# A gated linear-attention scan feeding a rational-activation MLP: one activation-table set, heads in pairs, other PSUM buffers

## The chip, the cores and the metric

The kernel runs on one core of a Trainium2 chip. A core has TensorE (PE, with its weight loads shown as PEld), VectorE (DVE), ScalarE (ACT), GpSimd (POOL) and SyncE (SP), which here only issues DMAs. The metric is the device time of one launch in microseconds; less is better.

## The reference

Inputs are `q`, `k`, `v`, `f_logit`, each of shape (4, 8, 768, 48) (batch B, heads H, sequence S, head width D), and the weights of an MLP with 384 inputs, 2048 inner and 384 outer columns.

```python
f = 1.0 / (1.0 + np.exp(-f_logit))
for t in range(S):
    state = f[:, :, t, :, None] * state + np.einsum('bhd,bhe->bhde', k[:, :, t], v[:, :, t])
    y[:, :, t] = np.einsum('bhd,bhde->bhe', q[:, :, t], state)
...
h = x @ w_in
P = a[0] + a[1] * h + a[2] * h2 + a[3] * h3          # h2 = h*h, h3 = h2*h
Q = 1.0 + np.abs(b[0]) * np.abs(h) + np.abs(b[1]) * h2
g = P / (Q + 1e-06)
out = g @ w_out
```

`x` is `y` with its heads side by side: 3072 tokens of 384 columns.

## The kernel before

The sequence is cut into NC = 6 chunks of C = 128 steps. A chunk is one attention stage over the 8 heads, then one expert stage on its 4 x 128 = 512 tokens. (The MLP is called the expert stage here.)

**Attention, per head.** `q`, `k`, `f_logit` are loaded from the queue of SP and `v` from that of POOL, all four batches side by side (BD = 192 columns). ACT forms `sig` (L104) and its logarithm `lsig` (L106). PE multiplies `lsig` by a triangular matrix U, a running sum over time, into `csT`, a part of the PSUM tile `psA` (L112); ACT takes its exponential with either sign, `AT` (L115) and `AinvT` (L117). DVE and POOL scale `q` and `k` with them (`qt_n` L120, `kt_n` L122); PE transposes both into `psB` (L126, L128, eight in all); DVE copies the results out (`qt_d` L131, `kt_d` L133). PE makes four column sums for the last decay (L136), of which ACT takes the exponential `alast` (L140); the scores (L144), which DVE masks (`sc_sb` L149); y from the masked scores and from the old state (L153, L157), which ACT copies out (`y_sb` L162) and SP stores to the HBM tensor `xT`; and `sv`, k times v (L168). DVE adds it to the state (`stmp` L173) and scales by `alast` (`state` L176). `csT`, the column sums and `sv` share the one buffer of `psA`.

**Expert stage, per chunk.** `xc` is read back from `xT` in three loads. For each of the KF = 16 blocks `m` of the inner columns, PE makes `h_ps` (L188, three matmuls), DVE casts it to `hb` (L192) and squares it (L194, shown as h), ACT makes `habs` (L196) and `pA` (L198), POOL makes `pB` (L201), DVE makes t (L204) and `Pp` (L206), POOL makes q (L208), DVE makes `Qq` (L211), ACT makes `lnQ` (L213) and `Qinv = exp(-lnQ)` (L215), and DVE makes `gall` (L216). Then, for each batch `sub`, 16 matmuls of `gall` with `w_out` go to `o_ps` (L220), ACT copies them out (L224) and SP stores them.

**Order.** The loops are unrolled. A scheduler at build time orders each engine's instructions, by priorities and by the buffers that each pool has; each engine then runs its own list in that order. So work of the next chunk can stand among that of this one. ACT holds one set of function tables at a time; where a function is not in the set, a table load (ACT_TABLE_LOAD) stands before it.

Of the kernel before, what the change touches and what calls it, by code (L numbers as in the profile page):

```python
# [8 lines left out]
F32 = mybir.dt.float32  # L9
BF16 = mybir.dt.bfloat16  # L10
# [5 lines left out]
def kernel(  # L16
# [12 lines left out]
    nc = tc.nc  # L29
# [4 lines left out]
    BC = B * C  # L34
    d_model = H * D
# [13 lines left out]
    for bb in range(B):  # L49
# [16 lines left out]
                                            ap=[[0, P]] + list(moe_b.ap)))  # L66
    babs = w_pool.tile([P, 2], F32)
    nc.scalar.activation(babs, b_sb, AF.Abs)

    with tc.tile_pool(name="attn_sb", bufs=3) as sb, \  # L70
         tc.tile_pool(name="attn_bf", bufs=3) as bf, \
         tc.tile_pool(name="ps_a", bufs=1, space=bass.MemoryType.PSUM) as ps_a, \
         tc.tile_pool(name="ps_b", bufs=1, space=bass.MemoryType.PSUM) as ps_b, \
         tc.tile_pool(name="ps_sc", bufs=1, space=bass.MemoryType.PSUM) as ps_sc, \
         tc.tile_pool(name="ps_y", bufs=1, space=bass.MemoryType.PSUM) as ps_y, \
         tc.tile_pool(name="ps_h", bufs=2, space=bass.MemoryType.PSUM) as ps_h, \
         tc.tile_pool(name="ps_o", bufs=2, space=bass.MemoryType.PSUM) as ps_o, \
# [8 lines left out]
      for c in range(NC):  # L86
        t0 = c * C
        for h in range(H):
            state = states[h]
            qn = sb.tile([C, BD], F32, tag="qn")  # L90
            kn = sb.tile([C, BD], F32, tag="kn")
            vn = bf.tile([C, BD], BF16, tag="vn")
            fn = sb.tile([C, BD], F32, tag="fn")
            nc.sync.dma_start(out=qn.rearrange("t (b d) -> t b d", b=B),
                              in_=q[:, h, t0:t0 + C, :].rearrange("b t d -> t b d"))
            nc.sync.dma_start(out=kn.rearrange("t (b d) -> t b d", b=B),
                              in_=k[:, h, t0:t0 + C, :].rearrange("b t d -> t b d"))
            nc.gpsimd.dma_start(out=vn.rearrange("t (b d) -> t b d", b=B),  # L98
                                in_=v[:, h, t0:t0 + C, :].rearrange("b t d -> t b d"))
            nc.sync.dma_start(out=fn.rearrange("t (b d) -> t b d", b=B),  # L100
                              in_=f_logit[:, h, t0:t0 + C, :].rearrange("b t d -> t b d"))

            sig = sb.tile([C, BD], F32, tag="sig")
            nc.scalar.activation(sig, fn, AF.Sigmoid)  # L104
            lsig = bf.tile([C, BD], BF16, tag="lsig")
            nc.scalar.activation(lsig, sig, AF.Ln)  # L106

            psA = ps_a.tile([C, 512], F32, tag="psA")
# [147 lines left out]
```

## Time and profile before

| | us |
|---|---|
| median of 6 runs (lowest to highest) | 875.47 (873.52 to 876.59) |
| the profiled execution, its time | 875.5 |
| its span from first to last instruction | 873.7 |
| ACT busy | 755.8 |
| PE / DVE / POOL busy | 441.9 / 363.3 / 219.6 |

The span is what the trace shows; 1.8 us of the time lie around it. An engine's busy time is a mean over two kinds of stage that alternate six times, so the stages are read apart. In a row of the timeline the first number is the start in us from the span's start, the second the length; in square brackets stands how long the engine had been idle before it and who ended that. A name such as `hb<-h_ps` says what is written from what.

### The profile page before, as it was taken

To read this page: it belongs to the slowest core of one execution; us is meant where nothing else is said; L and a number is where in the kernel's file an instruction comes from. 1 tells how busy PE (TensorE), PEld (TensorE's weight loads), DVE (VectorE), ACT (ScalarE), POOL (GpSimd) and SP (SyncE) were. 2 spreads that over 40 slices of the span, in tenths; PEclk is the share of its full clock that TensorE was granted. 3 is DMA by queue.
4 is the path that set the end of the run, shared out by engine and by line. 5 is a ranking of instruction groups with operands and counts; after the bars stand their busy time and mean duration, and the time that the engine had idled before them with its cause. 6 is when DMAs were issued, how large, how long until landed. Compare 5 with 4: busy or idle time off the path is not lost. (4 is left out here: it accounts for less than half of the span.)

```text
span 873.7 us, 7492 instructions
## 1 busy us (share of the span) xinstructions
PE 441.9 (51%) x2041; PEld 195.8 (22%) x2064; DVE 363.3 (42%) x873; ACT 755.8 (87%) x1012; POOL 219.6 (25%) x306
## 2 busy tenths in 40 slices
PE   0466544276644256664336664426665425755424
PEld 0243210043310024310013421103331102421001
DVE  0233655323554423365423364542345452345441
ACT  4888999868999968899978899996899996539994
POOL 3112432111432201252201243210233220224220
PEclk9999755565655565555556555556555556555556
DMA  9744100034300024400013420002430001200000
GB/s 161 102 65 68 20 0 1 17 73 61 48 2 0 0 55 70 69 8 0 0 29 66 66 40 1 0 0 66 68 51 3 1 0 48 39 19 0 1 0 36
DMA packets 127114, 29.59 MB, mean 34 GB/s; under 512 B 121569, under 2 KB 126689, under 8 KB 127073
## 3 DMA queue, kind: packets, MB, share of 16 engines
q1 hardware_dynamic: 99264, 23.61, 13.4%
q0 software_dynamic: 27808, 5.51, 7.3%
q8 instruction: 16, 0.26, 0.1%
q14 instruction: 26, 0.20, 0.1%
HBM read 27.53 MB, written 7.08 MB: 40 GB/s over the span
## 5 line engine op out<-in xcount | busy, mean ns | idle before, releaser
L220 PE MATMUL o_ps<-w_out_sb,gall 128*128 128x384 bf16 x384 | 116.7, 443 | 226.2 <-DVE gall L216 226.0
L188 PE MATMUL h_ps<-xc,w_in_sb 128*128 128x512 bf16 x265 | 125.7, 603 | 55.5 <-DVE hb L192 48.7
L201 POOL TENSOR_SCALAR pB<-hb,a_sb 128x512 bf16<-128x512 bf16 x96 | 78.4, 817 | 183.5 <-DVE Pp L206 143.7
L213 ACT ACT_TABLE_LOAD x90 | 115.5, 1283 | 1.6
L215 ACT ACT_TABLE_LOAD x90 | 115.5, 1283 | 1.6
L220 PEld LDWEIGHTS <-gall 128*128 128x128 bf16 x384 | 34.4, 112 | 336.1 <-DVE gall L216 315.1
L208 POOL TENSOR_SCALAR q<-h,babs 128x512 bf16<-128x512 bf16 x96 | 69.9, 729 | 112.5 <-DVE h L194 109.7
L98 POOL DMA_DIRECT2D vn<-in_v_dram x48 | 38.5, 802 | 230.3 <-PE y_ps L157 225.0
L216 DVE TENSOR_TENSOR gall<-Pp,Qinv 128x512 bf16<-128x512 bf16 x96 | 40.8, 425 | 116.1 <-ACT Qinv L215 115.7
L211 DVE TENSOR_TENSOR Qq<-q,habs 128x512 bf16<-128x512 bf16 x96 | 41.5, 433 | 95.9 <-ACT habs L196 95.3
L198 ACT ACTIVATE pA<-hb,a_sb 128x512 bf16<-128x512 bf16 x96 | 76.6, 798 | 0.0
L196 ACT ACTIVATE habs<-hb,babs 128x512 bf16<-128x512 bf16 x96 | 67.8, 707 | 6.0 <-DVE hb L192 6.0
L131 DVE COPY qt_d<-psB 48x512 bf16<-48x512 bf16 x48 | 20.0, 417 | 117.4 <-PE psB L128 83.7
L192 DVE CAST hb<-h_ps 128x512 bf16<-128x512 f32 x96 | 65.0, 683 | 6.7 <-PE h_ps L188 6.5
L126 PE MATMUL psB<-ident,qt_n 128*48 128x128 bf16 x192 | 49.0, 311 | 35.1 <-DVE qt_n L120 35.1
L153 PE MATMUL y_ps<-sc_sb,vn 128*48 128x128 bf16 x192 | 55.1, 287 | 19.1 <-DVE sc_sb L149 19.1
L188 PEld LDWEIGHTS <-w_in_sb 128*128 128x128 bf16 x288 | 35.5, 128 | 117.0 <-issue 114.8
L106 ACT ACT_TABLE_LOAD x47 | 60.3, 1283 | 0.8
L213 ACT ACTIVATE lnQ<-Qq 128x512 bf16<-128x512 bf16 x96 | 59.8, 628 | 1.0
L215 ACT ACTIVATE Qinv<-lnQ 128x512 bf16<-128x512 bf16 x96 | 59.8, 628 | 1.0
L104 ACT ACT_TABLE_LOAD x45 | 57.7, 1283 | 0.8
L157 PE MATMUL y_ps<-qt_d,state 48*48 48x128 bf16 x192 | 56.2, 293 | 0.0
(47 smaller groups left out, 702.3 us busy)
## 6 DMA issues: line engine op xcount, KB each, us to landing
qn<-in_q_dram SPq DMA_DIRECT2D x48, 96.0 KB, 2.6
kn<-in_k_dram SPq DMA_DIRECT2D x48, 96.0 KB, 2.5
fn<-in_f_logit_dram SPq DMA_DIRECT2D x48, 96.0 KB, 2.1
out_dram<-o_sb SPq DMA_DIRECT2D x24, 192.0 KB, 1.9
vn<-in_v_dram POOLq DMA_DIRECT2D x48, 48.0 KB, 2.9
xT_bridge<-y_sb SPq DMA_DIRECT2D x48, 48.0 KB, 2.3
xc<-xT_bridge SPq DMA_DIRECT2D x18, 128.0 KB, 2.6
w_in_sb<-in_moe_w_in_dram POOLq DMA_DIRECT2D x1, 1536.0 KB, 11.2
```

The lines of the kernel that those rows point to most:

```text
L104: nc.scalar.activation(sig, fn, AF.Sigmoid)
L106: nc.scalar.activation(lsig, sig, AF.Ln)
L157: nc.tensor.matmul(y_ps[:, b * C:(b + 1) * C], state[:, b * D:(b + 1) * D], qt_d[:, b * C:(b + 1) * C], start=False, stop=True)
L188: nc.tensor.matmul(h_ps, w_in_sb[:, kk, m * P:(m + 1) * P], xc[:, kk].rearrange("p b s -> p (b s)"), start=(kk == 0), stop=(kk == KD - 1))
L192: nc.vector.tensor_copy(hb, h_ps)
L196: nc.scalar.activation(habs, hb, AF.Abs, scale=babs[:, 0:1])
L198: nc.scalar.activation(pA, hb, AF.Identity, scale=a_sb[:, 3:4], bias=a_sb[:, 2:3])
L201: nc.gpsimd.tensor_scalar(pB, hb, a_sb[:, 1:2], a_sb[:, 0:1], op0=ALU.mult, op1=ALU.add)
L208: nc.gpsimd.tensor_scalar(q1, h2, babs[:, 1:2], 1.0 + 1e-6, op0=ALU.mult, op1=ALU.add)
L213: nc.scalar.activation(lnQ, Qq, AF.Ln)
L215: nc.scalar.activation(Qinv, lnQ, AF.Exp, scale=-1.0)
L220: nc.tensor.matmul(o_ps, gall[:, mm, sub * C:(sub + 1) * C], w_out_sb[:, mm, :], start=(mm == 0), stop=(mm == KF - 1))
```

## The change

1. One table set. Before the first activation `preload_act_table_set("natural_log_exp_and_others")` is called. `sig` is now exp(-f) and `lsig` is Ln(sig + 1), which is minus the old `lsig`; the signs of the three exponentials that follow are turned. Sigmoid is gone. The compiled program has 1 ACT_TABLE_LOAD row, where it had 315.
2. Heads in pairs. `qn`, `kn`, `vn`, `fn`, `sig`, `lsig`, `csT`, `AT`, `AinvT`, `qt_n`, `kt_n` are made for HG = 2 heads at once (GD = 384 columns); the loads stay one per head. The rest stays per head, in an inner loop over `j`.
3. Buffers. `attn_sb` has 2 instead of 3 buffers (of pairs); `AT` and `AinvT` move to a pool of their own with 3. `csT` has a PSUM bank of its own; the column sums and `sv` share a new one, `psS`. `ps_o` goes from 2 buffers to 1.
4. A constant `one_eps` is written and not used.

```diff
+    HG = 2
+    GD = HG * BD
...
+    nc.scalar.preload_act_table_set("natural_log_exp_and_others")
...
-    with tc.tile_pool(name="attn_sb", bufs=3) as sb, \
+    with tc.tile_pool(name="attn_sb", bufs=2) as sb, \
+         tc.tile_pool(name="attn_hb", bufs=3) as hsb, \
...
-         tc.tile_pool(name="ps_a", bufs=1, space=bass.MemoryType.PSUM) as ps_a, \
+         tc.tile_pool(name="ps_cs", bufs=1, space=bass.MemoryType.PSUM) as ps_cs, \
...
+         tc.tile_pool(name="ps_sv", bufs=1, space=bass.MemoryType.PSUM) as ps_sv, \
...
-         tc.tile_pool(name="ps_o", bufs=2, space=bass.MemoryType.PSUM) as ps_o, \
+         tc.tile_pool(name="ps_o", bufs=1, space=bass.MemoryType.PSUM) as ps_o, \
...
-        for h in range(H):
+        for hg in range(H // HG):
...
-            nc.scalar.activation(sig, fn, AF.Sigmoid)
+            nc.scalar.activation(sig, fn, AF.Exp, scale=-1.0)
...
-            nc.scalar.activation(lsig, sig, AF.Ln)
+            nc.scalar.activation(lsig, sig, AF.Ln, bias=1.0)
...
-            nc.scalar.activation(AT, csT, AF.Exp, scale=1.0)
+            nc.scalar.activation(AT, csT, AF.Exp, scale=-1.0)
...
+            for j in range(HG):
+                h = h0 + j
+                jo = j * BD
...
+                psS = ps_sv.tile([D, 512], F32, tag="psS")
+                alast_ps = psS[:, 0:B]
+                sv_ps = psS[:, 256:256 + BD]
```

Three places in the compiled order. First ACT, in the middle of an expert stage; one `m`, before:

```order
L213 ACT_TABLE_LOAD
L213 ACTIVATE lnQ<-Qq 128x512
L196 ACTIVATE habs<-hb,babs 128x512
L215 ACT_TABLE_LOAD
L215 ACTIVATE Qinv<-lnQ 128x512
L198 ACTIVATE pA<-hb,a_sb 128x512
```

And after, with one row of the next `m` behind it (L227 was L213, L210 was L196, L229 was L215, L212 was L198):

```order
L227 ACTIVATE lnQ<-Qq 128x512
L210 ACTIVATE habs<-hb,babs 128x512
L229 ACTIVATE Qinv<-lnQ 128x512
L212 ACTIVATE pA<-hb,a_sb 128x512
L227 ACTIVATE lnQ<-Qq 128x512
```

The four activations keep their order; the two loads are gone.

Second DVE, in the same place; before:

```order
L204 TENSOR_TENSOR t_974<-pA,h_966 128x512
L192 CAST hb<-h_ps 128x512
L206 TENSOR_TENSOR Pp<-t_974,pB 128x512
L211 TENSOR_TENSOR Qq<-q_1005,habs 128x512
L194 TENSOR_TENSOR h_1020<-hb 128x512
L216 TENSOR_TENSOR gall<-Pp,Qinv 128x512
```

After (L218, L206, L220, L225, L230, L208 for the same six operations):

```order
L218 TENSOR_TENSOR t_1000<-pA,h_992 128x512
L206 CAST hb<-h_ps 128x512
L220 TENSOR_TENSOR Pp<-t_1000,pB 128x512
L225 TENSOR_TENSOR Qq<-q_1031,habs 128x512
L208 TENSOR_TENSOR h_1046<-hb 128x512
L230 TENSOR_TENSOR gall<-Pp,Qinv 128x512
```

The six operations and their count stay; in most of the later blocks h and `gall` stand the other way round.

Third PE, in an attention stage, from the last score matmul of a head on; before:

```order
L144 MATMUL sc_ps<-qt_d,kt_d 128x128
L112 LDWEIGHTS U
L112 MATMUL psA<-lsig,U 128x192
L153 LDWEIGHTS vn
L153 MATMUL y_ps<-sc_sb,vn 48x128
L157 LDWEIGHTS state
L157 MATMUL y_ps<-qt_d,state 48x128
```

After:

```order
L159 MATMUL sc_ps<-qt_d,kt_d 128x128
L138 LDWEIGHTS qt_n
L138 MATMUL psB<-ident,qt_n 48x128
L140 LDWEIGHTS kt_n
L140 MATMUL psB<-ident,kt_n 48x128
L183 LDWEIGHTS kt_n
L183 MATMUL psS<-vn,kt_n 48x48
```

Before, y of the same head followed the scores, after the running sum of the next one. Now the transposes of the next head and `sv` of this one stand between the scores and y. In later chunks the column sums stand there too, just ahead of `sv`. Also on PE, one output matmul (L234, before L220) stands behind each block's three `h_ps` matmuls inside the expert stage, where two stood; 48 of a chunk's 64 follow after the stage, in groups of 16 among the matmuls of the next heads, where 32 did.

More of the change, by code (lines that the diff above doesn't have):

```diff
@@ L120 @@
             nc.vector.tensor_mul(qt_n, qn, AT)
[L121 removed]
+            kt_n = bf.tile([C, GD], BF16, tag="kt_n")
             nc.gpsimd.tensor_mul(kt_n, kn, AinvT)
[L124 to L129 removed]
```

151 lines of the change are left out of this document (76 added, 75 removed).

## The prediction

> **What bounds the kernel now.** I read the windows first, with one window on an attention stage (from the last `gall` of a chunk to the first `hb` of the next) and one on the expert stage that follows; the columns are stretch, length, busy time of PE, PEld, DVE, ACT, POOL, then granted clock, DMA share, GB/s. Above them stands the first line of the page.
>
> ```profile
> PE 441.9 (51%) x2041; PEld 195.8 (22%) x2064; DVE 363.3 (42%) x873; ACT 755.8 (87%) x1012; POOL 219.6 (25%) x306
> ...
> 452.40:509.70 57.30, 40.15 (x255) 23.52 (x257) 17.48 (x45) 45.04 (x73) 10.36 (x15) 0.56 0.43 71
> 509.70:592.50 82.80, 33.45 (x85) 8.96 (x87) 42.90 (x101) 81.91 (x99) 25.30 (x33) 0.52 0.03 4
> ```
>
> In the expert stage ACT is busy 81.91 of 82.80 us and nothing else above 42.90: ACT bounds it. In the attention stage ACT has 45.04 of 57.30, PE 40.15: neither is full, so a chain binds it. One chunk takes 140.1. The groups by line say what ACT does (count | busy, mean ns | idle before):
>
> ```profile
> L213 ACT ACT_TABLE_LOAD x90 | 115.5, 1283 | 1.6
> L215 ACT ACT_TABLE_LOAD x90 | 115.5, 1283 | 1.6
> ...
> L106 ACT ACT_TABLE_LOAD x47 | 60.3, 1283 | 0.8
> ...
> L104 ACT ACT_TABLE_LOAD x45 | 57.7, 1283 | 0.8
> ...
> L115 ACT ACT_TABLE_LOAD x41 | 52.6, 1283 | 0.7
> ```
>
> These five lines are 313 loads of 1.283 us, 402 of ACT's 755.8 us. The timeline of ACT (start, length) shows one `m` of the expert loop, and that of DVE the same loop later:
>
> ```profile
> 422.01 1.28 ACT L213 ACT_TABLE_LOAD   x1
> 423.30 0.63 ACT L213 ACTIVATE lnQ<-Qq 128x512 bf16<-128x512 bf16 x1
> 423.84 0.71 ACT L196 ACTIVATE habs<-hb,babs 128x512 bf16<-128x512 bf16 x1
> 424.56 1.28 ACT L215 ACT_TABLE_LOAD   x1
> 425.86 0.63 ACT L215 ACTIVATE Qinv<-lnQ 128x512 bf16<-128x512 bf16 x1
> 426.39 0.80 ACT L198 ACTIVATE pA<-hb,a_sb 128x512 bf16<-128x512 bf16 x1
> 427.21 1.28 ACT L213 ACT_TABLE_LOAD   x1
> ```
> ```profile
> 535.73 0.42 DVE L204 TENSOR_TENSOR t<-pA,h 128x512 bf16<-128x512 bf16 x1 [0.28 <-ACT pA L198]
> 536.08 0.69 DVE L192 CAST hb<-h_ps 128x512 bf16<-128x512 f32 x1
> 536.68 0.42 DVE L206 TENSOR_TENSOR Pp<-t,pB 128x512 bf16<-128x512 bf16 x1
> 538.36 0.42 DVE L211 TENSOR_TENSOR Qq<-q,habs 128x512 bf16<-128x512 bf16 x1 [1.27 <-ACT habs L196]
> 538.70 0.42 DVE L194 TENSOR_TENSOR h<-hb 128x512 bf16<-128x512 bf16 x1
> 540.23 0.42 DVE L216 TENSOR_TENSOR gall<-Pp,Qinv 128x512 bf16<-128x512 bf16 x1 [1.11 <-ACT Qinv L215]
> ```
>
> ACT repeats every 5.20 us (422.01 to 427.21) without a gap, two loads in each; DVE waits for it twice (1.27 before `Qq`, 1.11 before `gall`).
>
> The attention stage, one head, and then two `state` rows of the last chunk:
>
> ```profile
> 480.77 0.28 PE L136 MATMUL psA<-onesc_g,lsig 128*48 128x1 bf16 x4
> 481.44 0.30 PE L128 MATMUL psB<-ident,kt_n 128*48 128x128 bf16 x1 [0.39 <-POOL kt_n L122]
> 482.17 0.37 PE L168 MATMUL psA<-vn,kt_n 128*48 128x48 bf16 x4
> 482.42 0.42 DVE L131 COPY qt_d<-psB 48x512 bf16<-48x512 bf16 x1 [1.89 <-PE psB L128]
> 483.22 0.60 PE L144 MATMUL sc_ps<-qt_d,kt_d 48*128 48x128 bf16 x4 [0.68 <-DVE kt_d L133]
> 483.86 0.69 DVE L149 TENSOR_TENSOR sc_sb<-sc_ps,mask 128x512 bf16<-128x512 f32 x1 [0.44 <-PE sc_ps L144]
> 486.51 0.35 DVE L176 TENSOR_TENSOR state<-stmp,alast 48x192 bf16<-48x192 f32 x1 [1.96 <-PE y_ps L157]
> ...
> 763.40 0.35 DVE L176 TENSOR_TENSOR state<-stmp,alast 48x192 bf16<-48x192 f32 x1 [1.96 <-PE y_ps L157]
> 768.83 0.35 DVE L176 TENSOR_TENSOR state<-stmp,alast 48x192 bf16<-48x192 f32 x1 [1.96 <-PE y_ps L157]
> ```
>
> A head runs PE, DVE, PE, DVE in turn: transposes from 481.44 (end at 482.17, where L168 starts), copies, scores from 483.22, mask 483.86, y until 486.5. DVE waits for y 1.96 us with nothing to do, and PE waits for the copies and the mask. The `state` rows, one per head, come 5.43 apart in the last chunk; in the window above, seven of them (six of the chunk's heads and the first of the next) and the output matmuls share 57.3.
>
> **The change, part by part.**
>
> *Table loads.* The order has 315 load rows before and 1 after. ACT's `m` without its two loads is 5.20 - 2 x 1.28 = 2.64; since `lnQ` to `habs` steps 0.54 for a length of 0.63 where no load follows, two more such overlaps would give 2.45. I take 2.5 for ACT alone. The load row shows no drain around it: `pA` ends at 427.19, the load starts at 427.21, and `lnQ` starts 0.01 after the load before it. The Trainium skill (ScalarE: Activation LUTs, What ACT_TABLE_LOAD costs) puts a switch at about 2.66 us, 1283 ns of load and a drain of about 1380 ns. By it 314 removed loads would be worth 835 us of ACT, by the row 403; the trace agrees with the 1283 and shows no drain, so the row counts.
>
> *What is late next in the expert loop: DVE.* Six DVE operations per `m`, in the new order `t, hb, Pp, Qq, gall, h`. Start-to-start steps where DVE did not wait: t to hb 0.35, hb to Pp 0.60, Qq to h 0.34; the other three as the last. Sum 0.35 + 0.60 + 4 x 0.34 = 2.31. This is below ACT's 2.5. But POOL runs `pB` and `q` under it, and where DVE has no gaps the two disturb each other (first the spread of `pB`, ns min/median/max, then the start of an expert stage):
>
> ```profile
> L201 POOL TENSOR_SCALAR pB<-hb,a_sb x96: 752/762/1375, 89.9 to 848.3; 128x512 bf16<-128x512 bf16 x96
> ...
> 510.52 1.92 POOL L201 TENSOR_SCALAR pB<-hb,a_sb 128x512 bf16<-128x512 bf16 x2 [2.51 <-DVE hb L192]
> 512.42 1.77 POOL L208 TENSOR_SCALAR q<-h,babs 128x512 bf16<-128x512 bf16 x2
> ...
> 512.58 0.79 DVE L204 TENSOR_TENSOR t<-pA,h 128x512 bf16<-128x512 bf16 x1
> ```
>
> `pB` alone takes 0.76; two of them take 1.92 here, two `q` 1.77, and the DVE `t` under them 0.79 where its row above has 0.42. So a collision costs DVE about 0.4 and POOL up to 0.4. It does not touch `hb`, whose length stays 0.69 (it reads PSUM), so one of the two POOL operations of an `m` fits under `hb`'s 0.60; the other meets four back-to-back DVE operations. I charge one full collision, 0.48 (0.4, and 0.08 for the handoff): 2.31 + 0.48 = 2.8 per `m`. Bounds: 2.5 (no collision; ACT paces), and 3.2 (five DVE operations, 5 x 0.34, and two POOL operations, 2 x 0.76, never at once). The middle is nearest the row of 510.52.
>
> The Trainium skill (SBUF — State Buffer, Who interferes with whom) has this as an exclusive lock: a DVE instruction with two SBUF inputs and a GpSimd one that reads SBUF block each other in full. By that the bound of 3.2 would be the time per `m`; the rows agree with blocking, and its median of 762 ns says that a half-busy DVE leaves POOL its gaps.
>
> Sixteen `m` are 44.8 (16 x 2.8). Filling and draining the pipeline costs about 2.5 (a lone `hb`, `h`, `q` before the first `Qq`; `lnQ`, `Qinv`, `gall` after the last). By the order two heads of the next chunk now run inside the loop (one before); on a DVE without gaps each costs two copies at 0.42, the mask's 0.69, `stmp` and `state` at 0.35, 2.2 less 0.2 of overlap, so 4.0. Expert stage: 51, for 82.8.
>
> *Heads in pairs, transposes ahead.* PE's order becomes scores, transposes of the next head, `alast`, `sv`, y. The two copies (0.42 each) then lie under y, the mask (0.69) under the transposes. What remains in line: scores 0.60, eight transposes 0.83 (seven took 0.73), `alast` 0.28, its way through ACT about 0.3, `sv` 0.37, y 1.96, half a `csT` about 0.2: 4.54. I take 4.5. Bounds: 4.0, with the ACT handoff and drains hidden, and 5.4, the row of the last chunk, where the same serial chain ran with ACT's waits smallest. The pairing halves four ACT operations and `qt_n`/`kt_n` in number at twice the width; ACT and POOL are off the path here, so nothing. Eight loads per pair instead of four per head are the same bytes; DMA is at 0.43 of 57.3 us, that is 24.6 us of work in a stage of 43, still under it. New waits: a pair's `sig` needs both heads' `fn`, hidden by the second buffer; the store of y stands on SP behind loads that wait for a pair's buffer (rival C).
>
> *`ps_o` with one buffer.* Only one quarter of the output matmuls runs inside the expert loop; 48 instead of 32 come after it, and each 16 wait for ACT's copy of the previous 16.
>
> ```profile
> 454.55 6.45 PE L220 MATMUL o_ps<-w_out_sb,gall 128*128 128x384 bf16 x32
> ...
> 779.86 1.29 DVE L192 CAST hb<-h_ps 128x512 bf16<-128x512 f32 x2 [5.56 <-PE h_ps L188]
> ```
>
> The 32 took 6.45, 0.20 each; 48 are 9.7, and I charge 11 for a lower clock when heads stand between them. The separate `psS` bank lets `csT` go early; its cover is y. The last head's way through HBM to the first `hb` (5.56 of DVE idle in the last chunk) stays; I charge 5, since one next head fits into it.
>
> Attention stage: six heads 27 + 11 + 5 = 43, for 57.3.
>
> *Sum.* The start is bound by the first loads: the first `state` at 29.94, the first `hb` at 89.07, the last `gall` at 861.08.
>
> ```profile
> 29.94 0.35 DVE L176 TENSOR_TENSOR state<-stmp,alast 48x192 bf16<-48x192 f32 x1 [1.96 <-PE y_ps L157]
> ...
> 89.07 1.29 DVE L192 CAST hb<-h_ps 128x512 bf16<-128x512 f32 x2 [0.25 <-PE h_ps L188]
> ...
> 861.08 0.42 DVE L216 TENSOR_TENSOR gall<-Pp,Qinv 128x512 bf16<-128x512 bf16 x1 [3.00 <-ACT Qinv L215]
> ```
>
> After: 30 + 7 heads x 4.5 + 5.6 + 2 for the second head's loads = 69. Then 51; four chunks of 43 + 51 = 376; the last chunk, with no heads to interleave, 41 + 47 = 88; and the tail, 873.7 - 861.5 = 12.2 plus 16 matmuls of 0.20 = 15. Sum 599; the profiled execution took 875.5 for a span of 873.7, so 1.8 on top: 601. The median of the runs is 875.47, the same, so no shift.
>
> **The rivals.**
>
> A. ACT paces: POOL's two operations slip into waits of DVE and no collision costs. For it: ACT at 2.5 leaves DVE 0.2 of slack per `m`. Against: the row of 510.52. 96 `m` x 0.3 less: 572.
>
> B. The collision in full, 3.2 per `m`: 96 x 0.4 more: 639. For it: `pB` up to 1375 ns. Against: those are the extremes.
>
> C. Heads do not get below 5.4, because loads or the `alast`-`sv` handoff hold PE: 48 x 0.9 more: 644. For it: SP takes loads and stores in one row, and `alast` now sits between transposes and `sv`. Against: in this trace DMA is at 0.43.
>
> D. PE gets its full clock in the attention stage. The windows above have 0.56 and 0.52; PE would be busy 4.0 of 4.5. If PE's share shrank by a quarter: 48 x 1.0 less, 553. The Trainium skill (TensorE: Matmul & The Clock Gate, Part 1) has the clock released by one busy window of about 3.4 us. Against: the denser output matmuls release it here, the heads never did.
>
> E. The change does not do what it says, the functions keep switching tables: the expert stage stays at 82.8 and only heads gain, 601 + 6 x 32 = 793. Against: one load row in the order.
>
> F. Slower than before: on SP a pair's y stores stand behind loads whose buffers only a later pair frees, and PE stands still until `y_sb` is free, once for each of the 24 pairs. It decides from 274 / 24 = 11.4 us per pair, more than the pair's 9. At 12 us: 889. Against: three buffers for `y_sb`.
>
> **How the numbers follow.** My case 0.46, A 0.17, B 0.13, C 0.14, D 0.05, E 0.02, F 0.03. Predicted 601, its own range 580 to 625. With A, B and C inside, and the outer bounds of the head (4.0: 24 less) and of the ACT pace: 550 to 660, which leaves out E, F and the far ends of the others. 0.2% is about what a measurement of this kernel can tell. Faster by over 0.2%: all but F and a remainder, 0.96; same 0.01; slower 0.03.
>
> **What would show it.** ACT_TABLE_LOAD x1 and ACT busy near 335 (755.8 less 403 less some 20 for halved counts). `t` to `t` near 2.8 on DVE, its idle before `Qq` or `gall` small, `pB` and `q` means over 0.9 on POOL; 2.5 with ACT gapless would be A. `state` rows about 4.5 apart; 5.4 with PE waiting for ACT or a DMA would be C. First `hb` near 69. The prediction is wrong if a transfer, not an engine, ends the waits in the attention stage, or if the 48 output matmuls hold up the heads by much more than 11.

## The result, and the profile after

The kernel after takes 546.11 us (median of 8 runs, 544.57 to 547.70), the kernel before 875.57 in the same comparison (16 runs): a ratio of 0.624, 95% interval 0.6231 to 0.6249. The prediction was 601 with a range of 550 to 660: the direction and the terms of the expert stage held; the time came out 55 us lower, just under the range. The profiled execution has a span of 544.6 us.

The page of the kernel after, busy time by engine:

```profile
PE 393.0 (72%) x2022; PEld 182.5 (33%) x2040; DVE 365.7 (67%) x850; ACT 323.6 (59%) x602; POOL 267.0 (49%) x282
```

Its groups of instructions (count | busy, mean ns | idle before and what ended it):

```profile
L215 POOL TENSOR_SCALAR pB<-hb,a_sb 128x512 bf16<-128x512 bf16 x96 | 120.8, 1258 | 81.3 <-DVE hb L206 46.8 <-DVE Pp L220 33.4 <-DVE gall L230 0.8
...
L222 POOL TENSOR_SCALAR q<-h,babs 128x512 bf16<-128x512 bf16 x96 | 82.1, 856 | 6.0 <-DVE h L208 6.0
...
L218 DVE TENSOR_TENSOR t<-pA,h 128x512 bf16<-128x512 bf16 x96 | 60.5, 631 | 3.6 <-ACT pA L212 3.6
L227 ACT ACTIVATE lnQ<-Qq 128x512 bf16<-128x512 bf16 x96 | 60.0, 628 | 26.9 <-DVE Qq L225 26.6
...
L69 ACT ACT_TABLE_LOAD x1 | 1.3, 1283 | 0.7 <-PEq L254 0.7
```

One table load is left, ACT's busy time has fallen from 755.8 to 323.6, and no engine is above 72%. `t` on DVE now takes 631 ns on the mean, `pB` on POOL 1258; and ACT waits 26.6 us in all for DVE's `Qq`. Those three say that DVE paces the expert loop, held up by POOL. One `m` in the timeline of DVE, then the same of POOL, shows it (start, length):

```profile
260.45 0.68 DVE L206 CAST hb<-h_ps 128x512 bf16<-128x512 f32 x1
261.05 0.41 DVE L220 TENSOR_TENSOR Pp<-t,pB 128x512 bf16<-128x512 bf16 x1
261.38 0.41 DVE L225 TENSOR_TENSOR Qq<-q,habs 128x512 bf16<-128x512 bf16 x1
261.72 0.41 DVE L230 TENSOR_TENSOR gall<-Pp,Qinv 128x512 bf16<-128x512 bf16 x1
262.05 0.41 DVE L208 TENSOR_TENSOR h<-hb 128x512 bf16<-128x512 bf16 x1
262.39 0.83 DVE L218 TENSOR_TENSOR t<-pA,h 128x512 bf16<-128x512 bf16 x1
263.13 0.68 DVE L206 CAST hb<-h_ps 128x512 bf16<-128x512 f32 x1
```
```profile
260.23 0.85 POOL L222 TENSOR_SCALAR q<-h,babs 128x512 bf16<-128x512 bf16 x1
261.64 1.31 POOL L215 TENSOR_SCALAR pB<-hb,a_sb 128x512 bf16<-128x512 bf16 x1 [0.55 <-DVE Pp L220]
262.92 0.85 POOL L222 TENSOR_SCALAR q<-h,babs 128x512 bf16<-128x512 bf16 x1
```

From `hb` to `hb` it is 2.68 us here; the median from `t` to `t` is 2.69. `pB` starts while DVE is in `Qq` and lasts through `gall` and `h`; `t`, which starts under it, takes 0.83; `q` then runs under `hb`. One DVE operation per `m` loses 0.41.

The windows, an expert stage and the attention stage behind it (the columns as before):

```profile
163.90:214.20 50.30, 33.36 (x111) 11.31 (x113) 46.09 (x105) 41.15 (x71) 36.05 (x35) 0.53 0.13 19
214.20:244.20 30.00, 28.48 (x206) 16.40 (x207) 14.26 (x34) 10.39 (x26) 7.04 (x9) 0.78 0.61 106
```

PE is busy 28.48 of 30.00 us in the attention stage, at a granted clock of 0.78 (before: 40.15 of 57.30, at 0.56). Last, `state` and the first `hb` of two chunks on DVE:

```profile
231.66 0.35 DVE L191 TENSOR_TENSOR state<-stmp,alast 48x192 bf16<-48x192 f32 x1 [1.75 <-PE y_ps L172]
...
234.75 0.35 DVE L191 TENSOR_TENSOR state<-stmp,alast 48x192 bf16<-48x192 f32 x1 [0.64 <-PE y_ps L172]
...
237.95 0.35 DVE L191 TENSOR_TENSOR state<-stmp,alast 48x192 bf16<-48x192 f32 x1 [0.86 <-PE y_ps L172]
...
242.15 0.35 DVE L191 TENSOR_TENSOR state<-stmp,alast 48x192 bf16<-48x192 f32 x1 [1.53 <-PE y_ps L172]
...
244.19 1.29 DVE L206 CAST hb<-h_ps 128x512 bf16<-128x512 f32 x2 [0.56 <-PE h_ps L202]
...
483.46 1.29 DVE L206 CAST hb<-h_ps 128x512 bf16<-128x512 f32 x2 [5.52 <-PE h_ps L202]
```

The first three `state` rows are 3.1 and 3.2 apart, the fourth 4.2. Before the first `hb` DVE idles 0.56 us in this chunk and 5.52 only in the last, which has no next heads to run.

Stage by stage, summed over the chunks (first `hb` to last `gall`; last `gall` to next first `hb`; the tail is what follows the last `gall`):

| us | start | 6 expert stages | 5 attention stages | tail | span |
|---|---|---|---|---|---|
| before | 89.1 | 493.2 | 278.8 | 12.6 | 873.7 |
| predicted | 69 | 302 | 213 | 15 | 599 |
| after | 78.1 | 286.0 | 164.0 | 16.5 | 544.6 |

### The profile page after: what moved, and what is told of

Same layout as the page of the kernel before. It is cut to its first block, busy times and chain, and to the rows that moved or that the text cites. A ratio compares the mean times of both kernels' runs of the same rounds, so it can differ in the third digit from the quotient of the medians.

```text
span 544.6 us, 6851 instructions
## 1 busy us (share of the span) xinstructions
PE 393.0 (72%) x2022; PEld 182.5 (33%) x2040; DVE 365.7 (67%) x850; ACT 323.6 (59%) x602; POOL 267.0 (49%) x282
## 4 chain that ended last, share of the span: by engine, by line
PE 38%; DVE 35%; issue 10%; ACT 5%; SPq 4%; POOL 3%; DMA 3%; DVEq 0%; POOLq 0%; ACTq 0%
PE o_ps L234 11%; DVE t L218 9%; PE y_ps L172 7%; PE y_ps L168 6%; DVE gall L230 6%; DVE Pp L220 6%; DVE h L208 5%; PE sc_ps L159 4%; PE psB L138 3%; DVE hb L206 3%; PE psB L140 3%; DVE Qq L225 3%; SPq L106 2%; PE psS L183 2%; POOL q L222 2%
## 5 line engine op out<-in xcount | busy, mean ns | idle before, releaser
L215 POOL TENSOR_SCALAR pB<-hb,a_sb 128x512 bf16<-128x512 bf16 x96 | 120.8, 1258 | 81.3 <-DVE hb L206 46.8
L234 PE MATMUL o_ps<-w_out_sb,gall 128*128 128x384 bf16 x384 | 108.1, 404 | 21.8 <-DVE gall L230 19.7
L222 POOL TENSOR_SCALAR q<-h,babs 128x512 bf16<-128x512 bf16 x96 | 82.1, 856 | 6.0 <-DVE h L208 6.0
L212 ACT ACTIVATE pA<-hb,a_sb 128x512 bf16<-128x512 bf16 x96 | 76.7, 799 | 0.0
L234 PEld LDWEIGHTS <-gall 128*128 128x128 bf16 x384 | 41.2, 110 | 105.2 <-DVE gall L230 74.2
L227 ACT ACTIVATE lnQ<-Qq 128x512 bf16<-128x512 bf16 x96 | 60.0, 628 | 26.9 <-DVE Qq L225 26.6
L177 ACT CAST y_sb<-y_ps 48x512 bf16<-48x512 f32 x48 | 27.7, 577 | 73.8 <-PE y_ps L172 72.7
L210 ACT ACTIVATE habs<-hb,babs 128x512 bf16<-128x512 bf16 x96 | 67.9, 707 | 6.1 <-DVE hb L206 6.0
L206 DVE CAST hb<-h_ps 128x512 bf16<-128x512 f32 x96 | 64.6, 679 | 8.0 <-PE h_ps L202 8.0
L218 DVE TENSOR_TENSOR t<-pA,h 128x512 bf16<-128x512 bf16 x96 | 60.5, 631 | 3.6 <-ACT pA L212 3.6
L229 ACT ACTIVATE Qinv<-lnQ 128x512 bf16<-128x512 bf16 x96 | 58.6, 614 | 0.1
L129 POOL TENSOR_TENSOR kt_n<-kn,AinvT 128x384 bf16<-128x384 f32 x24 | 24.1, 1003 | 67.6 <-ACT AinvT L124 61.1
L191 DVE TENSOR_TENSOR state<-stmp,alast 48x192 bf16<-48x192 f32 x48 | 18.2, 380 | 52.0 <-PE y_ps L172 51.9
L164 DVE TENSOR_TENSOR sc_sb<-sc_ps,mask 128x512 bf16<-128x512 f32 x48 | 33.0, 688 | 21.6 <-PE sc_ps L159 21.0
L238 ACT COPY o_sb<-o_ps 128x384 f32<-128x384 f32 x24 | 11.4, 476 | 60.7 <-PE o_ps L234 58.5
L225 DVE TENSOR_TENSOR Qq<-q,habs 128x512 bf16<-128x512 bf16 x96 | 41.3, 430 | 7.6 <-POOL q L222 7.6
L230 DVE TENSOR_TENSOR gall<-Pp,Qinv 128x512 bf16<-128x512 bf16 x96 | 44.0, 458 | 0.5 <-ACT Qinv L229 0.2
```

The source lines that it names most:

```text
L206: nc.vector.tensor_copy(hb, h_ps)
L210: nc.scalar.activation(habs, hb, AF.Abs, scale=babs[:, 0:1])
L212: nc.scalar.activation(pA, hb, AF.Identity, scale=a_sb[:, 3:4], bias=a_sb[:, 2:3])
L215: nc.gpsimd.tensor_scalar(pB, hb, a_sb[:, 1:2], a_sb[:, 0:1], op0=ALU.mult, op1=ALU.add)
L218: nc.vector.tensor_mul(t1, pA, h2)
L222: nc.gpsimd.tensor_scalar(q1, h2, babs[:, 1:2], 1.0 + 1e-6, op0=ALU.mult, op1=ALU.add)
```

## The experiments

Times are compared with the 546.1 of the kernel after, those of the kernel before lying between 874.2 and 876.5 in each comparison. The stage sums in the text are read in the same way as in the table above.

### One part of the change at a time

**The table set alone**, in the kernel before:

```diff
+    nc.scalar.preload_act_table_set("natural_log_exp_and_others")
...
-            nc.scalar.activation(sig, fn, AF.Sigmoid)
+            nc.scalar.activation(sig, fn, AF.Exp, scale=-1.0)
...
```

> The kernel before with the one table set alone (heads single, PSUM banks and buffers as before). My theory: the expert stage falls from 82.8 to about 50 us as in the kernel after, because only the loads held it: 6 x 33 = 197 us less. The attention stage gains less than the changed kernel's 57 to 33: with single heads and no transposes ahead it stays near 50. Sum 875 - 197 - 5 x 7 = about 640. Rival: the loads are nearly the whole gain, the attention stage falls to 33 to 40 as well, because the loads before `sig`, `lsig` and `AT` sat in the head's chain: about 560 to 580.

598.2 us, ratio 0.6844 (0.6833 to 0.6855): between the two. The expert stages fall to 281.2, the attention stages only to 219.3, so the loads carry 276 of the 328 us, and a head goes from 6.6 to 5.4. Its rows on PE say what holds the 5.4:

```profile
336.27 0.28 PE L137 MATMUL psA<-onesc_g,lsig 128*48 128x1 bf16 x4 [0.64 <-ACT AinvT L118]
...
340.12 0.60 PE L145 MATMUL sc_ps<-qt_d,kt_d 48*128 48x128 bf16 x4 [0.68 <-DVE kt_d L134]
...
341.64 0.28 PE L137 MATMUL psA<-onesc_g,lsig 128*48 128x1 bf16 x4 [0.64 <-ACT AinvT L118]
```

PE stands idle 0.64 before the column sums (`psA` L137), waiting for ACT to have read `AinvT` out of the same PSUM bank, and 0.68 before the scores (L145), waiting for a copy.

**Pairs, banks and buffers alone**, the loads back:

```diff
-    nc.scalar.preload_act_table_set("natural_log_exp_and_others")
...
-            nc.scalar.activation(sig, fn, AF.Exp, scale=-1.0)
+            nc.scalar.activation(sig, fn, AF.Sigmoid)
...
```

> The changed kernel with Sigmoid and Ln in place of the one set, so that the loads are back: pairs, PSUM banks and buffers alone. My theory: the expert stage is ACT's again at about 83 us, the heads lose the loads only where two heads share them, and the attention stage falls from 57 to about 45: 875 - 5 x 12 - 10 = about 805. Rival: heads and loads hinder each other on ACT (a head's loads stand in the expert loop as well), and the attention stage does not fall: about 860 to 880.

791.0, ratio 0.9046 (0.9032 to 0.9059). The expert stages are 502.1 again, the attention stages 187.2. So this half of the change is worth 83 us where the loads are still there, and 52 (598.2 to 546.1) where they are not: paired heads also share loads, of which this kernel has 254 for 315.

**The whole change without the pairs:**

```diff
-    HG = 2
+    HG = 1
```

> The changed kernel with HG = 1: one table set, the new PSUM banks and buffers, but each head by itself. Theory (the clock and the banks make the short heads): the `state` rows stay 3.1 apart at full clock and 4.2 at half, and the time is 546 plus what twice as many small ACT operations cost in the expert stage, at most 10 us: 546 to 560. Rival (transposing both heads of a pair at once is what shortens a head): heads about 5 apart, 48 x 1 more: about 595.

558.7, ratio 0.6398 (0.6375 to 0.6421): the pairs themselves are worth 12.6, and the rest of the second half, banks and buffers, 39.5.

**The same with the shared bank back**, as in the kernel before:

```diff
-            csT = ps_cs.tile([C, GD], F32, tag="csT")
+            psA = ps_cs.tile([C, 512], F32, tag="csT")
+            csT = psA[:, 0:GD]
...
-                alast_ps = psS[:, 0:B]
-                sv_ps = psS[:, 256:256 + BD]
+                alast_ps = psA[0:D, GD:GD + B]
+                sv_ps = psA[0:D, 256:256 + BD]
```

> One table set and single heads as in the run with HG = 1 (558.7), but with the column sums and `sv` back in the bank of `csT`, as in the kernel before. Theory: the own bank is what takes a head from 5.4 (one set alone, 598.2) towards 4.4, because `alast`'s column sums wait there until `AinvT` has read the bank (0.64 of PE idle before them in the run with the set alone): 585 to 600. Rival: the run of 48 output matmuls (one `ps_o`) makes the difference through the clock, and it is still there: 560 to 570.

599.5, ratio 0.6842 (0.6833 to 0.6852). All of the 40 us go with that one bank; heads are back at 5.4, the attention stages at 44.8 each but the last. PE's two waits are back as well: in the five attention stages it stands 22.4 us before the column sums, for `AinvT`, and 16.0 before the scores, for a copy, and it idles 44.1 us in all (16.6 in the kernel with the own bank). So the wait at the bank itself is only about half of the 40; the rest goes with the order that the bank allows. The one-buffer `ps_o`, which this kernel keeps, does not help the heads.

### PE's clock and the output matmuls

**Three quarters of the output matmuls left out:**

```diff
-        for sub in range(B):
+        for sub in range(1):
...
+            for s4 in range(B):
+                nc.sync.dma_start(out=out[s4 * S + t0: s4 * S + t0 + C, :], in_=o_sb)
```

> The changed kernel with the output matmuls of batch 0 alone, whose result is stored for all four batches (three quarters of the output product are left out). In the changed kernel 16 of them take 4.65 us cold and 2.77 after. Clock theory: the run of 48 is what releases PE's clock, and the heads behind it run at 3.1 instead of 4.2 only for that reason. Without it PE gets full clock for a few us per chunk at most, and the heads stay near 4.2: 4 heads x 1.1 back per chunk. So of the removed 10.2 us per chunk (4.65 + 2.77 + 2.77) only about 6 are gained: 546 - 6 x 6 = about 510. Rival: the heads are short because the loads are gone, whatever stands ahead of them; `state` rows 3.1 apart, and the whole 61 us are gained: 485.

514.3, ratio 0.5884 (0.5875 to 0.5894), near the clock theory. First the window of the attention stage that follows the first expert stage, then three `state` rows of the next on DVE:

```profile
125.40:151.50 26.10, 25.69 (x178) 15.43 (x179) 14.18 (x37) 10.48 (x28) 8.13 (x10) 0.50 0.67 104
```
```profile
212.55 0.35 DVE L191 TENSOR_TENSOR state<-stmp,alast 48x192 bf16<-48x192 f32 x1 [1.72 <-PE y_ps L172]
...
216.88 0.35 DVE L191 TENSOR_TENSOR state<-stmp,alast 48x192 bf16<-48x192 f32 x1 [1.63 <-PE y_ps L172]
...
221.06 0.35 DVE L191 TENSOR_TENSOR state<-stmp,alast 48x192 bf16<-48x192 f32 x1 [1.71 <-PE y_ps L172]
```

PE is busy 25.69 of 26.10 us at a clock of 0.50, as in the four other attention stages, and heads are 4.2 to 4.3 apart. Some 51 us of matmuls (5 x 10.2) left the attention stages, and these fell by only 17.9, to 146.1: 33 went back into slower heads, a few of them for the one head more that finishes there (32 for 31). Less the waits before the first `hb` (7.3), a head takes 4.34 on the mean here (138.8 by 32).

**Two `ps_o` banks again**, one `ps_h` in exchange:

```diff
-         tc.tile_pool(name="ps_h", bufs=2, space=bass.MemoryType.PSUM) as ps_h, \
-         tc.tile_pool(name="ps_o", bufs=1, space=bass.MemoryType.PSUM) as ps_o, \
+         tc.tile_pool(name="ps_h", bufs=1, space=bass.MemoryType.PSUM) as ps_h, \
+         tc.tile_pool(name="ps_o", bufs=2, space=bass.MemoryType.PSUM) as ps_o, \
```

> The changed kernel with two `ps_o` banks again and one `ps_h` bank in exchange. By its order about 38 of the 64 output matmuls of a chunk follow the last `h_ps` instead of 51. My prediction charged the longer run with a loss of 4.5 per chunk; by that this kernel gains some 20: 525. Clock theory: the longer run is what holds PE's clock through the heads behind it; with the shorter one the release ends earlier, heads go back towards 4.3, and the stage gets no shorter although 2 to 3 us of output matmuls leave it: 546 to 560. Rival: one `ps_h` bank slows the expert loop (h_ps waits for `hb`), the stage grows from 47.6: then the loss stands in the expert stages, not in the attention stages.

533.6, ratio 0.6083 (0.6071 to 0.6095). Windows of 3.42 us from within the run of 32 output matmuls on:

```profile
211.88:215.30 3.42, 3.42 (x15) 1.77 (x14) 0.00 (x0) 0.04 (x1) 0.00 (x0) 0.64 0.58 109
215.30:218.72 3.42, 3.42 (x35) 2.17 (x33) 0.39 (x1) 1.30 (x4) 0.00 (x0) 1.00 0.51 114
218.72:222.14 3.42, 3.42 (x36) 2.29 (x32) 2.79 (x8) 2.03 (x6) 0.85 (x2) 0.85 0.56 131
222.14:225.56 3.42, 3.42 (x28) 2.28 (x27) 1.95 (x6) 1.56 (x4) 1.72 (x2) 0.50 1.09 121
```

And two `state` rows behind it:

```profile
228.17 0.35 DVE L191 TENSOR_TENSOR state<-stmp,alast 48x192 bf16<-48x192 f32 x1 [1.53 <-PE y_ps L172]
...
232.35 0.35 DVE L191 TENSOR_TENSOR state<-stmp,alast 48x192 bf16<-48x192 f32 x1 [1.51 <-PE y_ps L172]
```

The clock half of the theory holds: the release lasts about 7 us (within the first window to within the third; by the clock that the trace records, 6.8 to 10.2 over the five stages, 13.7 to 17.1 in the kernel after), and the heads behind it are back at 4.2. Its conclusion does not: the kernel is 12.5 faster. The attention stages lose 11.7 and the tail 4.7, since 15 output matmuls per chunk move into the expert stage (30 start in it, 15 in the kernel after), where PE has time; the expert stages pay 4.8 for the one `ps_h` bank. So the longer release gives back only a part of what the longer run costs.

**PE made denser in the expert stage:**

```diff
-            for kk in range(KD):
-                nc.tensor.matmul(h_ps, ...)
+            for rr in range(2):
+                for kk in range(KD):
+                    nc.tensor.matmul(h_ps, ...)
```

> The changed kernel with every group of three `h_ps` matmuls issued twice (the first pass is overwritten), so that PE is denser in the expert stage. One pass takes 1.44 beside half-clock rows, two and the one or two output matmuls per `m` 3.4 at half clock and 1.7 at full. Clock theory: PE is released within the expert stage, the first 16 output matmuls take 2.8 instead of 4.65 and more heads run at 3.1: 6 x 2 + up to 5 x 4 less, 515 to 535. Rival 1: PE is released for a few us now and then, falls back, and paces the loop at half clock with 3.4 per `m`: 546 + 96 x 0.7 = 613. Rival 2: released, but heads unchanged because the clock falls again before them: 540 to 546.

566.4, ratio 0.6464 (0.6453 to 0.6474): slower, and none of the three. The clock is released there, as the window of an expert stage shows, and it is lost again before the output matmuls, as two rows of PE show:

```profile
165.40:214.10 48.70, 30.35 (x142) 12.67 (x142) 45.25 (x102) 40.56 (x67) 34.07 (x32) 0.92 0.07 13
```
```profile
210.00 0.50 PE L235 MATMUL o_ps<-w_out_sb,gall 128*128 128x384 bf16 x1 [3.85 <-DVE gall L231]
...
218.40 4.58 PE L235 MATMUL o_ps<-w_out_sb,gall 128*128 128x384 bf16 x16
```

With 0.92 of clock the loop is no shorter (284.7 for 286.0), since DVE paces it. At its end PE idles 3.85 us, and the first sixteen output matmuls take 4.58, as cold as ever. The 20 us come from the attention stages (184.7): seven heads finish in each of the first four, eight and five in turn in the kernel after, and the clock in them is 0.67 to 0.73. How much is the order and how much the clock, this run does not tell.

### The collision of DVE and POOL

**`pB` out of the loop** (a constant tile instead):

```diff
+    nc.vector.memset(pB0, 0.25)
...
-            pB = msb.tile([P, NT], BF16, tag="pB")
-            nc.gpsimd.tensor_scalar(pB, hb, a_sb[:, 1:2], a_sb[:, 0:1],
-                                    op0=ALU.mult, op1=ALU.add)
...
-            nc.vector.tensor_add(Pp, t1, pB)
+            nc.vector.tensor_add(Pp, t1, pB0)
```

> The changed kernel with POOL's `pB` left out of the loop (a constant tile stands in for a0 + a1 h; that term is not computed). One `m` takes 2.69 us in the changed kernel, `t` 0.83 in it, and ACT without waits would need 2.47 (steps 0.53 + 0.62 + 0.52 + 0.80). Theory: the 0.41 that `t` loses is the collision with `pB`, which has stood since four DVE operations; without it `t` takes 0.42, ACT paces at 2.47, and 96 x 0.22 = 21 are gained: 525. Rival 1: `q`, which starts with `t`, collides just as well: `t` stays 0.8, 546. Rival 2: the period comes from the handoffs between ACT and DVE: `t` falls, the period does not: 546.

511.6, ratio 0.5839 (0.5829 to 0.5849). **`q` off POOL** (`bratio` is |b0|/|b1|):

```diff
+    nc.vector.tensor_mul(bratio, babs[:, 0:1], binv)
...
-            nc.scalar.activation(habs, hb, AF.Abs, scale=babs[:, 0:1])
+            nc.scalar.activation(habs, hb, AF.Abs, scale=bratio)
...
-            nc.gpsimd.tensor_scalar(q1, h2, babs[:, 1:2], 1.0 + 1e-6,
-                                    op0=ALU.mult, op1=ALU.add)
...
-            nc.vector.tensor_add(Qq, q1, habs)
+            nc.vector.tensor_add(Qq, h2, habs)
...
-            nc.scalar.activation(lnQ, Qq, AF.Ln)
+            nc.scalar.activation(lnQ, Qq, AF.Ln, scale=babs[:, 1:2], bias=one_eps)
```

> The changed kernel with `q` taken off POOL: `Qq` becomes the sum of h squared and `habs` (scaled by |b0|/|b1|), and `lnQ` multiplies by |b1| and adds 1 + 1e-6 with its own scale and bias. ACT and DVE have the same instructions as before, POOL one fewer per `m`. Theory 1: the collision is `pB`'s, 2.69 stays or `t` is met by `pB` alone: 540 to 548. Theory 2: any second POOL operation would do it, and with `q` gone `pB` moves under `hb`: `t` 0.42, period 2.47, 525. Theory 3: `lnQ` with pointers takes longer than 0.63 (`pA` with two pointers has 0.80): ACT 2.64 without waits, and at most 5 are gained: 541.

520.4, ratio 0.5936 (0.592 to 0.5951). **Both**, no POOL operation in the loop:

> Both of the two before at once: no POOL operation in the expert loop (a0 + a1 h is not computed). This is the price of sharing with POOL altogether. Theory: `t` 0.42, six DVE operations 2.31, ACT paces with 2.47, or 2.64 if `lnQ` with pointers takes 0.80: 525 or 541. If the time does not fall below 540 although `t` does, ACT is the bound and the collision costs next to nothing.

505.4, ratio 0.5776 (0.5759 to 0.5793); 40.7 less, half of it in the expert stages. The line of `t` in the three, in this order (ns min/median/max):

```profile
L217 DVE TENSOR_TENSOR t<-pA,h x96: 406/415/836, 82.5 to 493.1; 128x512 bf16<-128x512 bf16 x96
```
```profile
L222 DVE TENSOR_TENSOR t<-pA,h x96: 403/491/836, 82.5 to 500.9; 128x512 bf16<-128x512 bf16 x96
```
```profile
L221 DVE TENSOR_TENSOR t<-pA,h x96: 403/414/426, 82.4 to 485.1; 128x512 bf16<-128x512 bf16 x96
```

Without `pB`, `t` is at 415 ns on the median though `q` still runs; with neither it never exceeds 426. Without `q` the median is 491, but it hides two groups: 38 of the 96 take over 600 (50 in the kernel after), as these two in a row show:

```profile
168.45 0.82 DVE L222 TENSOR_TENSOR t<-pA,h 128x512 bf16<-128x512 bf16 x1
...
171.14 0.82 DVE L222 TENSOR_TENSOR t<-pA,h 128x512 bf16<-128x512 bf16 x1
```

They are still 2.69 apart, which is also the median of the run. So in this order of operations it is `pB` that collides, with or without `q`: the first of the three theories for the run without `q`, although its time is nearest that of the second. The expert stages are 251.7, 278.3 and 264.1: 34.3, 7.7 and 21.9 less. The first is more than the 21 expected, because ACT without waits turned out at 2.36 per `m`, not 2.47, as two `lnQ` rows of the first of these kernels show:

```profile
245.32 0.62 ACT L226 ACTIVATE lnQ<-Qq 128x512 bf16<-128x512 bf16 x1
...
247.68 0.62 ACT L226 ACTIVATE lnQ<-Qq 128x512 bf16<-128x512 bf16 x1
```

The second is still paced by DVE, at 2.69. The third is held by ACT, at 2.54 from `lnQ` to `lnQ`: `lnQ` with its two pointers takes 802 ns there, and 811 in the second, for 628. The Trainium skill (ScalarE: Activation LUTs, What ACT_TABLE_LOAD costs) gives some 93 ns for each pointer operand; the trace agrees with two of them, 0.17 to 0.18. In the second and third the attention stages are 18 and 20 us shorter, though as many heads (31) finish in them. The order differs: 154 transposes and 70 score matmuls start in these stages, 213 and 108 in the kernel after, so the front half of some heads now runs inside the expert stages. How much of the 18 and 20 us this makes is not measured.

**`pB` moved to DVE**, nothing left out:

```diff
-            nc.gpsimd.tensor_scalar(pB, hb, a_sb[:, 1:2], a_sb[:, 0:1],
+            nc.vector.tensor_scalar(pB, hb, a_sb[:, 1:2], a_sb[:, 0:1],
```

> The changed kernel with `pB` moved from POOL to DVE, nothing left out. Without `pB` on POOL `t` fell to 0.42 and an `m` to ACT's pace (2.47) in an earlier run, 511.6. DVE needs 2.31 for its six operations; the seventh has one bf16 input and two pointers. Theory: it takes 0.2 to 0.34, DVE 2.5 to 2.65 per `m`, expert stages 43 to 45: 515 to 530. Rival: with pointers it takes 0.7 as `hb` does, DVE 3.0 per `m`, slower than the collision it removes: 570 or more.

578.3, ratio 0.6606 (0.6593 to 0.6618): the time of the rival. But not by its reason, as two rows of the same operation show, with the POOL rows of `q` beside them:

```profile
178.04 0.41 DVE L215 TENSOR_SCALAR pB<-hb,a_sb 128x512 bf16<-128x512 bf16 x1
...
193.43 0.79 DVE L215 TENSOR_SCALAR pB<-hb,a_sb 128x512 bf16<-128x512 bf16 x1
```
```profile
178.29 1.05 POOL L222 TENSOR_SCALAR q<-h,babs 128x512 bf16<-128x512 bf16 x1 [2.23 <-DVE h L208]
...
193.33 0.73 POOL L222 TENSOR_SCALAR q<-h,babs 128x512 bf16<-128x512 bf16 x1 [2.24 <-DVE h L208]
```

Where `pB` starts ahead of `q` it takes 0.41 and `q` 1.05; where `q` is ahead, `q` takes 0.73 and `pB` 0.79. So the pointers are not the price: the collision found another victim, and the one that starts second pays. Of the 32 us that the kernel loses, though, only 9.5 lie in the expert stages (295.5); 20.7 lie in the attention stages (184.7), in the first four of which seven heads finish each. So the last test keeps `pB` on DVE and folds `q` into `lnQ`, with the edits of both kernels above:

> Nothing left out: `pB` on DVE and `q` folded into `lnQ`, so that POOL has no operation in the expert loop. With `pB` on DVE alone, its first rows took 0.41 and the later ones 0.78, all beside POOL's `q`; `t` was back at 0.41. Theory (any POOL operation that runs under back-to-back DVE work costs one DVE operation 0.4, whichever stands there): with POOL silent `pB` takes 0.41 throughout, DVE needs 2.31 + 0.34 = 2.65 per `m`, ACT 2.64 (with `lnQ` at 0.81), expert stages near 46, and the time is 510 to 520. Rival (`pB` on DVE takes 0.78 by itself once the loop runs, because of its pointers): DVE 3.0 per `m` as with `pB` on DVE alone, 550 to 575.

```profile
L219 DVE TENSOR_SCALAR pB<-hb,a_sb x96: 400/403/409, 79.6 to 527.2; 128x512 bf16<-128x512 bf16 x96
```

`pB` is at 404 ns on the mean in all 96, `t` at 413, and the expert stages are 264.0, 44.0 each where near 46 were expected. Yet the time is 549.5, ratio 0.6274 (0.6265 to 0.6282): the attention stages went from 164.0 to 187.5 and took all of it back. Seven heads finish in each of the first four, where the kernel after alternates eight and five, and more of the heads' work starts in the five stages (258 transposes and 132 score matmuls for 213 and 108). With two `ps_o` banks added:

> No POOL operation in the loop (`pB` on DVE, `q` in `lnQ`: 549.5) with two `ps_o` banks and one `ps_h`. That kernel's expert stages were the shortest that leave nothing out (44.0 on the mean), but its attention stages 37.5 instead of 32.8, with seven heads in each where the changed kernel has five or eight. Theory: the order of the heads is at fault, and another set of banks gives another order: near 520. Rival: only the 12.5 of the banks, 537.

533.2, ratio 0.6086 (0.607 to 0.6102), a gain of 16.3, nearer to the rival; attention stages 164.9. Where the heads stand in the order decides here as much as what the loop costs, and no run isolates it.

### The start, and the gains together

**The weights' loads behind the first pair's:**

```diff
-    w_in_sb = w_pool.tile_from(...)
-    w_out_sb = w_pool.tile_from(...)
...
+            if c == 0 and hg == 1:
+                w_in_sb = w_pool.tile_from(...)
+                w_out_sb = w_pool.tile_from(...)
```

> The changed kernel with the loads of `w_in` and `w_out` issued behind those of the first pair of heads. In the changed kernel `sig` waits 14.3 us for the first pair's `fn`, and the first `state` stands at 38.1 (29.9 before). Theory: those two loads (1.5 MB each) share the 16 DMA engines with the first pairs; behind them the first `state` comes near 28, the first `hb` near 70 instead of 78, and 8 us stay gained to the end: 538. Rival: the start is bound by the bytes of all loads (DMA share 0.90 up to the first `hb`), the second and third pair wait as long as the first does now, and the first `hb` stays at 76 to 78: 544 to 547.

542.3, ratio 0.6196 (0.6184 to 0.6208): 3.8 less, half of what was hoped. The first and the third `state`:

```profile
17.95 0.35 DVE L192 TENSOR_TENSOR state<-stmp,alast 48x192 bf16<-48x192 f32 x1 [1.13 <-PE y_ps L173]
...
42.41 0.35 DVE L192 TENSOR_TENSOR state<-stmp,alast 48x192 bf16<-48x192 f32 x1 [1.05 <-PE y_ps L173]
```

The first pair is 20 us earlier (17.95 for 38.11), but the third head comes at 42.41, when the second came in the kernel after (42.23): the weights now stand ahead of its loads. With `pB` on DVE as well:

> Both edits at once: the weights' loads behind the first pair's, and `pB` on DVE. They touch different parts (the start and the expert stages), so the gains should add: by the theories 546 - 8 - 25 = 513; if the start is bound by bytes and `pB` takes 0.7 on DVE, 570.

577.7, ratio 0.6599 (0.6588 to 0.661), the same as with `pB` on DVE alone. And with `q` off POOL:

> The two edits that gained, together, nothing left out: `q` off POOL (520.4 alone) and the weights' loads behind the first pair's (542.3 alone, 3.8 under the changed kernel). They act in different stages, so the gains should add: 520.4 - 3.8 = 517. Rival: the earlier start is used up, because the first `hb` is bound by the bytes of all loads and the planner orders the heads otherwise: 519 to 522.

519.6, ratio 0.5945 (0.5932 to 0.5959), not to be told from 520.4. The first `hb` is 2.7 us earlier than in that kernel, and nothing that can be measured is left of it at the end: the expert stages are 6.4 shorter, the attention stages 7.1 longer. The best version that leaves nothing out has the three edits that gained:

> The three edits that gained, together, nothing left out: `q` folded into `lnQ`, the weights' loads behind the first pair's, and two `ps_o` banks with one `ps_h`. Theory: the last gave 12.5 under the changed kernel, in the attention stages and the tail, the first two 519.6; they act in different places: 519.6 - 12.5 = 507. Rival: with ACT pacing the loop at 2.65 the single `ps_h` bank shows (`hb` waits for `h_ps`), and half of the gain is lost: 513.

516.9, ratio 0.5909 (0.5896 to 0.5922), 29 us under the kernel after. The attention stages are 143.1, but the expert stages 286.2: `hb` waits 15.2 us in all for `h_ps`, 8.0 in the kernel after, and the gain of 2.7 over the last kernel is even less than the rival's.

## Why the prediction was right and wrong, by its steps

- **Table loads: right.** One row is left and ACT's busy time is 323.6, for 335 predicted. ACT without waits was put at 2.5 per `m`; the run without `pB` paces at 2.36. Of the 403 us of loads, 276 are the gain by themselves, 212 of it in the expert stages and 60 in the attention stages: those in the heads lay partly beside other work.
- **2.8 per `m`, DVE with one collision: right in mechanism, 2.69 in size.** `t` lost 0.41; the 0.08 for the handoff was not needed. That it is one collision, not two or none, is shown by the runs without `pB`, without `q` and without either. By the rule of the Trainium skill that the prediction cited (SBUF — State Buffer, Who interferes with whom) both would block each other in full, 3.2 per `m`; the trace has blocking, `t` 0.41 longer and `pB` 1.31 for 0.75, but with `q` under `hb` only one of the two costs DVE time.
- **Expert stage 51: 47.7 on the mean.** 16 x 2.69 is 43.0; the filling, draining and interleaved heads cost 4.6 where 6.5 were charged. Six stages: 16 of the 55 us.
- **Attention stage 43: 32.8 on the mean. This is the step that failed**, 49 of the 55 us, in three of its terms. *The 5 us to the first `hb`* were one row of the last chunk, charged in every chunk. The waits after are 0.25 to 0.56 in the next three stages, 0.73 in the fourth and 5.52 in the last, 7.3 in sum where I charged 25. The trace of before had it: the quoted row of its first chunk shows 0.25. *The head at 4.5* was a serial chain in which PE waits for ACT and the mask. The own bank took those waits away (40 us by the run with the shared bank), PE became nearly gapless, and a gapless head takes 4.2 at half clock. *The clock*: by the run with a quarter of the output, heads behind the full run are cheaper by most of 33 us because the clock stays released, down to 3.1. Together: 31 heads took 105.7 us (164.0 less 5 x 10.2 and 7.3) where I charged 133 for 30 (213 less 55 and 25). By size, 18 of the 49 are the waits, 4 the output matmuls (51 for 55), and 27 the heads. These 27 are nearly all the clock's: all PE terms of my sum were rows at half clock, and at half clock, in the run with a quarter of the output, a head takes 4.34 on the mean. So 4.5 was close in size for half clock, though by another chain than the one I added up; what failed in it is the assumption that PE stays at half clock.
- **The clock as a rival, D (553): closest in time, and its argument against was half right.** The heads do not release the clock. The output matmuls do, and the heads behind them then run in it. That 553 lies so near 546 is partly chance: it took 48 us off the heads, of which the clock gave about 29 (31 heads at 3.41 for 4.34), and the rest of the 55 came from the waits, the output matmuls and the expert stages, less what the start and the tail took back.
- **Rival C, heads at 5.4:** what the new set alone gives. It did not come about because of the bank, which I had costed at nothing ("its cover is y"). My step from 5.4 to 4.5 was put down to the pairs and the transposes ahead; the runs give the pairs 12.6 us and the bank 40.
- **`ps_o` with one buffer: right in sign, about half in size.** 48 matmuls take 10.2, not 11; I charged 4.5 per chunk over the 32 of before; against two banks the run shows 12.5 us in all, 2.1 per chunk, or 2.9 without the 4.8 that it pays for the one `ps_h` bank.
- **First `hb` at 69: 78.1.** The second head's loads were charged 2 us. The first `state` came 8.2 later (38.11 for 29.94), since `sig` now waits for two heads' loads (with single heads and the rest of the change it stands at 32.07, and the first `hb` at 73.0); but ten heads had finished by then, which shortened the stages behind it. With the tail this gave back 11 of the 65 us that the stages gained on the prediction.
- **Tail 15: 16.5.** Its first sixteen matmuls ran cold.

## What to carry to other kernels

A PSUM bank that two stages of one chain share is a wait, even if each use is short: here the engine idled 0.64 before it in a head, and an own bank was worth 40 us, about half of it that wait and the rest the order that it allowed. A charge read from one row of a special chunk (the first, the last) has to be checked against the other chunks before it is multiplied. And where DVE has no gaps left, one POOL operation cost one DVE operation 0.4 us, as much as it takes alone; moving `pB` to DVE only chose another one. Free of it were the loops without POOL, and the one whose only POOL operation, `q`, mostly ran under `hb`.

## What the runs showed of the hardware that was not expected

PE's busy time does not tell what its clock will be. Windows of 3.42 us in the attention stage of the kernel after:

```profile
216.18:219.60 3.42, 3.42 (x13) 1.57 (x11) 1.54 (x2) 0.06 (x1) 0.99 (x1) 0.50 0.80 181
219.60:223.02 3.42, 3.42 (x22) 1.92 (x21) 0.82 (x2) 1.06 (x2) 0.59 (x1) 1.00 0.43 106
...
226.44:229.86 3.42, 2.48 (x26) 1.56 (x24) 1.56 (x4) 0.48 (x1) 0.00 (x0) 1.00 0.68 185
...
233.28:236.70 3.42, 3.24 (x33) 2.03 (x32) 2.78 (x9) 1.52 (x4) 1.85 (x3) 0.99 0.56 81
236.70:240.12 3.42, 3.42 (x27) 2.19 (x26) 1.93 (x6) 1.58 (x4) 0.65 (x1) 0.50 1.02 127
240.12:243.54 3.42, 3.42 (x25) 2.00 (x24) 1.89 (x5) 1.52 (x4) 1.35 (x2) 0.50 0.44 82
```

A window full of output matmuls (13 rows, 3.42 busy) is followed by full clock; windows just as full of head matmuls (27 and 25 rows) stay at 0.50. The release survives a window of 2.48 busy and ends behind one of 3.24, after 17.1 us; in the kernel with two `ps_o` banks it ends after about 7 with PE busy all the time. The Trainium skill (TensorE: Matmul & The Clock Gate, Part 1) names a busy window of about 3.4 us for the release; the first rows agree with it, the full windows of head matmuls do not. It names an idle window for the return, and none stands ahead of 236.70. What ends the release is open, but it goes with the output matmuls: over the five attention stages it ended 4.3 to 9.2 us after the last of their run, with two `ps_o` banks 3.3 to 7.4, in the kernel before 2.6 to 3.1.
